# Split weights, an added mask and VectorE differences in a chain of an mLSTM layer and two feed-forward layers

## The chip, the core and the metric

The kernel runs on one core of a Trainium2 chip. The metric is the device time in microseconds (us). One execution was also profiled; its span runs from the first to the last instruction of the core.

## What is computed

The first stage is an mLSTM over 2 batches, 8 heads, 768 steps and 40 values a head. The kernel takes it in chunks of 128 steps: with the running maximum in hand, each chunk is a masked matrix of decays times scores, plus what the state carried into it. Two feed-forward layers follow, each 320 to 2048 to 320, all in float32.

```python
m_new = np.maximum(f_gate[:, :, t] + m, i_gate[:, :, t])
C = f_stab * C + i_stab * einsum('bhd,bhe->bhde', vt, kt)
y[:, :, t] = sigmoid(o_gate) * (C @ qt) / max(|n . qt|, 1)
x = y as (1536, 320)
h = x @ w_in;  g = h - tanh(h);  x = g @ w_out
h = x @ w_in2; g = h * tanh(softplus(h)); out = g @ w_out2
```

## The kernel before, in words

**Float32 products in parts.** Each float32 operand is held as a rounded high part and a low part, the difference of the two; a product is high x high, high x low and low x high. A weight tile holds 128 of the 2048 hidden columns: columns 0 to 255 are the first 256 input rows as two 128x128 blocks, columns 256 to 575 are the output weights, and columns 576 to 703 are the last 64 of the 320 input rows, put there twice, in partitions 0 to 63 and again in 64 to 127. `conv_w` makes the tile: two VectorE steps and a ScalarE step put the raw bits right (L202, L210, L214; L204 and L207 in the second layer), ScalarE rounds all 704 columns (L217), and VectorE writes the low parts in two pieces: 576 columns on 128 partitions (L220), then 128 columns on partitions 64 to 127 only (L221). That second piece overwrites the doubled rows' high parts, so that one 128x128 block holds high over low. The first tile's pieces run on GpSimd.

`transpose_x` makes xT for a chunk's activations: three transposes on TensorE, one rounding copy on ScalarE (L290, 128x3x128), one low part on VectorE (L293, 128x3x128). `mm1` then issues 8 matmuls a weight tile, and `mm2` 3 for each 128 tokens (L649 to L651).

**The order of work.** Layer 1 has 6 blocks of 2 chunks. The program walks a list of 48 tiles of layer 1: each block's first weights (8 for block 0, 10 for the others), then each block's rest. `attend` feeds the mLSTM of the next block in between, `lead1` the conversion of weights. A scheduler then sets each engine's order from priorities and buffers; the instructions of an engine run in that order. `with after(...)` adds order edges.

**A tile of layer 1** (`tile1`): two tanh and a square on ScalarE (L608 to L610), two products on VectorE (L613, L614), ReLU on ScalarE (L615), a predicated copy on VectorE (L617), and in `split_g` the rounding gh on ScalarE (L597) and the low part gl on GpSimd (L598). Layer 2 has the same difference on VectorE (L630).

**The mLSTM's mask.** `attention` builds the exponent of the decays in PSUM (nb) and takes its exponential on ScalarE into Dm (L361). For chunk 0 the causal mask is a further product into nb (L353: identity times cm, which is 2^100 above the diagonal), and the exponential of its negative is 0. For all later chunks GpSimd's affine_select (L363) zeroes Dm behind the exponential. VectorE then multiplies Dm by the scores (L389).

**Rows of gates.** `gates` scans all 768 steps. `rest_n` splits the rows of n and i of chunks 1 to 5 (640 columns of 16 partitions) into high parts on ScalarE (L163 from `copy_r`) and low parts on VectorE (L525), in the tile nr; from there small DMAs bring a chunk's rows to md and sd, which the product of L358 reads.

**Buffers.** The pool wp has 16 slots (tag "w"), first used by the gates' rows; the pool xp has 5 (tag "x") for the first 4 raw weight tiles and then xT.

Of the kernel before, what the change touches and what calls it, by code (L numbers as in the profile page):

```python
# [8 lines left out]
F32 = mybir.dt.float32  # L9
F32R = mybir.dt.float32r  # L10
U32 = mybir.dt.uint32
# [14 lines left out]
def kernel(  # L26
# [20 lines left out]
    HP = P // 2  # L47
    REM0, REM1 = 256 + DM, 256 + DM + 128
    HI0, HI1, OUT_HI, PCH = 0, 128, 256, REM0
    LO0, LO1, OUT_LO = WC, WC + 128, WC + 256  # L50
    WT = WC + 256 + DM

# [62 lines left out]
    EC = 1  # L115
    nr = once.tile([P, S - EC * L], F32R, name="nr")

# [56 lines left out]
    def load_w(n=1):  # L174
        for _ in range(n):
            if pending_loads:
                layer, f = pending_loads.pop(0)
                early = layer == 0 and f < ER
                t = (xp if early else rawp).tile(
                    [P, 2 * WC], U32, tag="x" if early else "raw", name="raw", bufs=NB - 1 if early else None  # L180
                )
                queued(
                    lambda: nc.sync.dma_start(out=t, in_=(w1, w2)[layer][f].bitcast(U32)), layer == 0 and f < CUT[0]
                )
                raw[layer, f] = t
# [3 lines left out]
    def conv_w(layer, f, first=(), behind=()):  # L189
# [29 lines left out]
        with after(scored[NP + 1] if (layer, f) == (0, CUT[0] - 1) else []):  # L219
            eng.tensor_tensor(w[:, WC:WT], in0=zf[:, 0:REM0], in1=wf[:, 0:REM0], op=ALU.subtract)  # L220
        lows[layer, f] = eng.tensor_tensor(w[64:P, REM0:REM1], in0=zf[64:P, REM0:REM1], in1=wf[64:P, REM0:REM1], op=ALU.subtract)  # L221
        wtile[layer, f] = w
# [54 lines left out]
    def new_xT(layer, bi):  # L277
        nt = len(blk[layer, bi]) * L
        p, m = (late.get("x", xp), M1) if layer == 0 else (x2pool(bi), M2)
        t = p.tile([P, 2, 3, m], F32R, tag="x", name="xT", bufs=len(supers[0]) if layer else 1 if p is not xp else NB - 1)  # L280
        xT[layer, bi] = tuple(t[:, n, :, 0:nt] for n in range(2))

    def transpose_x(layer, bi, pos):
        j = blk[layer, bi][pos]
        src = xo[:, j, :]
        t_ps = at_ps([P, 3, P], "xt")
        for n in range(3):
            x = nc.tensor.transpose(t_ps[:, n, :], src[:, n * P:(n + 1) * P], ident)  # L288
        hi, lo = (t[:, :, pos * L:(pos + 1) * L] for t in xT[layer, bi])
        chain[:] = [x, nc.scalar.activation(out=hi, in_=t_ps, func=AF.Copy)]  # L290

        def low():
            chain.append(nc.vector.tensor_tensor(lo, in0=t_ps, in1=hi.bitcast(F32), op=ALU.subtract))  # L293

        return low
# [23 lines left out]
    def attention(j):  # L319
# [18 lines left out]
        for hf in range(2):  # L338
# [18 lines left out]
            else:  # L357
                nc.tensor.matmul(flat, lhsT=sds[b], rhs=md_[:, hf].rearrange("p g s -> p (g s)"), start=True, stop=True)  # L358
# [109 lines left out]
    def gates():  # L468
# [45 lines left out]
        def rest():  # L514
            with after([first]):
                scans(L, S)
            return rest_n

        def rest_n():
            for n, t in enumerate((n_t, i_t)):  # L520
                t, hi, lo = t[:, EC * L:S], nr[64 * n:64 * n + BH], nr[64 * n + 32:64 * n + 32 + BH]
                with after(texp):
                    copy_r(0, hi, t)
                with after([lows[0, 1]]):
                    nc.vector.tensor_tensor(lo, in0=t, in1=hi.bitcast(F32), op=ALU.subtract)  # L525
            return rest_u
# [36 lines left out]

    segs = [(bi, 0, CUT[bi]) for bi in range(NB)] + [(bi, CUT[bi], NF) for bi in range(NB)]
    tiles = [(0, bi, f) for bi, f0, f1 in segs for f in range(f0, f1, NP)]
    half = len(tiles)
# [8 lines left out]
    def mm1(i):  # L575
        l, bi, fs, nt = span(i)
        t = ps_h.tile([P, MX], F32, tag="h", name="h")[:, 0:len(fs) * nt]
        xh, xl = xT[l, bi]
        pairs = [
            (HI0, xh, 0), (HI1, xh, 1), (HI0, xl, 0), (HI1, xl, 1), (LO0, xh, 0), (LO1, xh, 1), (PCH, xh, 2), (PCH, xl, 2),  # L580
        ]
        for k, f in enumerate(fs):
            w = wtile[l, f]
            for n, (o, x, kk) in enumerate(pairs):
                with after([] if n else hold):
# [47 lines left out]
    def mm2(i):  # L633
# [18 lines left out]
        if fs[-1] + 1 in ends_ or fs[-1] == NF - 1:  # L652
            more = l == 0 and fs[-1] + 1 > CUT[bi]
            for t, a in enumerate(accs.pop((l, bi))):
# [21 lines left out]
    late = {}  # L676

# [5 lines left out]
    def program():  # L683
# [297 lines left out]
```

## Time and profile before

| | us |
|---|---|
| median of 3 runs | 448.72 (448.59 to 448.79) |
| the profiled execution's own time | 447.9 |
| its span | 446.2 |
| TensorE busy in the span | 436.4 |
| VectorE busy | 305.4 |
| ScalarE busy | 283.5 |
| GpSimd busy | 99.2 |

In the profile PE is TensorE's matmuls, PEld its weight loads, DVE VectorE, ACT ScalarE, POOL GpSimd. L12 is line 12 of the kernel before. Matmuls overlap in the records, so a busy TensorE is not one at its peak; w_ps are matmuls on constants that nobody reads. The chain of waits follows the last instruction back to what released it, step by step. A window's row gives the busy time of each engine in that stretch.

### The profile page before, as it was taken

How to read it: one execution, taken by the hardware profiler on the slowest of the kernel's cores; microseconds unless marked ns; L12 is line 12 of the kernel's file. 1: busy time of each engine (PE TensorE's matmuls, PEld its weight loads, DVE VectorE, ACT ScalarE, POOL GpSimd, SP SyncE). 2: the span in 40 equal slices, each digit the busy share in tenths (PEclk: the TensorE clock that was granted, in tenths of full speed). 3: DMA queues.
4: the chain of work that ended last, by engine and by line, in shares of the span. 5: the costliest groups of instructions: out<-in, count | busy, mean ns of one | idle time of the engine just before them, and what ended most of it. 6: DMA issues, size and time to landing. Idle time of an engine off the chain costs nothing.

```text
span 446.2 us, 7979 instructions
## 1 busy us (share of the span) xinstructions
PE 436.4 (98%) x3114; PEld 399.5 (90%) x3114; DVE 305.4 (68%) x521; ACT 283.5 (64%) x519; POOL 99.2 (22%) x107
## 2 busy tenths in 40 slices
PE   9899989999999999999999999999999999999996
PEld 5657979899899999999999999999999888999996
DVE  7899999978899896578999987898522211211112
ACT  6687987485786858889889877666434322333331
POOL 2307235343452521333333331000000000000000
PEclk9999999999999999999999999999999999999999
DMA  8986526423244210002222110543010000100001
GB/s 247 368 301 206 187 62 226 125 70 95 62 151 136 66 67 0 1 2 66 65 67 66 65 66 0 195 132 128 0 60 0 1 1 1 42 18 0 1 0 59
DMA packets 22728, 38.03 MB, mean 85 GB/s; under 512 B 1348, under 2 KB 17028, under 8 KB 22692
## 3 DMA queue, kind: packets, MB, share of 16 engines
q1 hardware_dynamic: 22692, 37.54, 25.7%
q8 instruction: 24, 0.39, 0.4%
q14 instruction: 12, 0.10, 0.1%
HBM read 35.41 MB, written 1.97 MB: 84 GB/s over the span
## 4 chain that ended last, share of the span: by engine, by line
PE 86%; DVE 8%; ACT 4%; issue 1%; ACTq 0%; DVEq 0%
PE h L586 37%; PE acc L649 12%; PE acc L651 12%; PE acc L650 12%; PE pv L409 3%; PE sc L385 2%; PE w_ps L690 2%; PE it L396 2%; PE xt L288 2%; DVE g L613 1%; DVE t L614 1%; DVE g L617 1%; DVE Dm L389 1%; ACT raw L210 1%; PE nb L358 1%
## 5 line engine op out<-in xcount | busy, mean ns | idle before, releaser
L586 PE MATMUL h<-xT,w 128*128 128x256 f32 (+1 forms) x1152 | 205.8, 321 | 0.5 <-DVE w L220 0.2
L586 PEld LDWEIGHTS h<-xT,w 128*128 128x128 f32 x1152 | 168.7, 188 | 15.7 <-issue 0.9
L649 PE MATMUL acc<-w,gh 128*128 128x320 f32 x384 | 119.5, 312 | 0.6 <-ACT gh L597 0.4
L650 PE MATMUL acc<-w,gh 128*128 128x320 f32 x384 | 118.8, 310 | 0.0
L651 PE MATMUL acc<-w,gl 128*128 128x320 f32 x384 | 114.0, 310 | 0.0
L598 POOL TENSOR_TENSOR gl<-g,gh 128x512 fp32r<-128x512 f32 x48 | 62.5, 1303 | 139.1 <-ACT gh L597 134.1
L630 DVE TENSOR_TENSOR gl<-g,gh 128x512 fp32r<-128x512 f32 x48 | 33.2, 691 | 87.4 <-ACT g L629 87.2
L628 ACT ACTIVATE gh<-h 128x512 fp32r<-128x512 f32 x48 | 28.7, 598 | 78.1 <-PE h L586 78.0
L649 PEld LDWEIGHTS acc<-w,gh 128*128 128x128 f32 x384 | 72.2, 188 | 3.4 <-ACT gh L597 0.7
L650 PEld LDWEIGHTS acc<-w,gh 128*128 128x128 f32 x384 | 72.2, 188 | 2.4
L651 PEld LDWEIGHTS acc<-w,gl 128*128 128x128 f32 x384 | 70.4, 188 | 0.7 <-issue 0.4
L617 DVE COPY_PREDICATED g<-u,t 128x512 f32<-128x512 uint32 x48 | 39.3, 824 | 10.0 <-ACT u L615 9.6
L597 ACT ACTIVATE gh<-g 128x512 fp32r<-128x512 f32 x48 | 30.3, 632 | 22.8 <-DVE g L617 21.5
L613 DVE TENSOR_TENSOR g<-u,h 128x512 f32<-128x512 f32 x48 | 32.7, 680 | 13.8 <-ACT u L610 3.9
L615 ACT ACTIVATE u<-u,bias 128x512 f32<-128x512 f32 x48 | 34.8, 725 | 8.2 <-DVE g L613 8.2
L217 ACT ACTIVATE w<-raw 128x704 fp32r<-128x704 f32 x32 | 27.2, 861 | 10.8 <-DVE raw L214 10.5
L614 DVE TENSOR_TENSOR t<-h,t 128x512 f32<-128x512 f32 x48 | 32.8, 684 | 0.0
L214 DVE SCALAR_TENSOR_TENSOR raw<-raw 128x704 uint32<-128x704 uint32 x32 | 32.0, 1007 | 1.0 <-ACT raw L207 0.4
L220 DVE TENSOR_TENSOR w<-raw,w 128x576 fp32r<-128x576 f32 x31 | 29.1, 939 | 1.9 <-ACT w L217 1.8
L610 ACT ACTIVATE u<-u 128x512 f32<-128x512 f32 x48 | 30.4, 636 | 0.0
L608 ACT ACTIVATE u<-h 128x512 f32<-128x512 f32 x48 | 28.1, 585 | 1.3 <-PE h L586 1.3
L629 ACT ACTIVATE g<-h 128x512 f32<-128x512 f32 x48 | 28.5, 594 | 0.0
(108 smaller groups left out, 445.0 us busy)
## 6 DMA issues: line engine op xcount, KB each, us to landing
raw<-in_w_dram SPq DMA_DIRECT2D x32, 704.0 KB
qk_t<-in_qk_dram SPq DMA_DIRECT2D x12, 512.0 KB
kv_t<-in_kv_dram SPq DMA_DIRECT2D x12, 324.0 KB
out_dram<-xo SPq DMA_DIRECT2D x12, 160.0 KB
xo<-in_og_dram SPq DMA_DIRECT2D x2, 800.0 KB
xo<-in_og_dram SPq DMA_DIRECT2D x1, 320.0 KB
sd<-nr SPq DMA_DIRECT2D x20, 4.0 KB
md<-nr SPq DMA_DIRECT2D x10, 8.0 KB
```

The lines of the kernel that those rows point to most:

```text
L214: third[layer, f] = nc.vector.scalar_tensor_tensor(z, in0=z, scalar=3, in1=lo32, op0=ALU.logical_shift_left, op1=ALU.bitwise_or)
L586: y = nc.tensor.matmul(t[:, k * nt:(k + 1) * nt], lhsT=w[:, o:o + P], rhs=x[:, kk, :], start=(n == 0), stop=(n == len(pairs) - 1),)
L598: nc.gpsimd.tensor_tensor(gl, in0=g, in1=gh.bitcast(F32), op=ALU.subtract)
L610: squared[:] = [nc.scalar.activation(out=u, in_=u, func=AF.Square, scale=G_SA)]
L613: mark[:] = [nc.vector.tensor_tensor(g, in0=u, in1=h, op=ALU.mult)]
L614: nc.vector.tensor_tensor(t, in0=h, in1=t, op=ALU.subtract)
L615: relus[i] = nc.scalar.activation(out=u, in_=u, func=AF.Relu, bias=bias[:, 0:1])
L617: chosen[i] = nc.vector.copy_predicated(out=g, mask=u.bitcast(U32), data=t)
L630: mark.append(nc.vector.tensor_tensor(gl, in0=g, in1=gh.bitcast(F32), op=ALU.subtract))
L649: turn(lambda: nc.tensor.matmul(a, lhsT=gh[:, sl], rhs=wh, start=(f in ends_), stop=False))
L650: turn(lambda: nc.tensor.matmul(a, lhsT=gh[:, sl], rhs=wl, start=False, stop=False))
L651: turn(lambda: nc.tensor.matmul(a, lhsT=gl[:, sl], rhs=wh, start=False, stop=end))
```

## The change

Four edits. (1) The last 64 rows: the weight tile now rounds all 704 columns and writes one low part of all 704, on 128 partitions (high blocks HI0, HI1, PCH; low blocks LO0, LO1, PCL); xT holds five blocks rather than six, and the third holds the high part in partitions 0 to 63 and the low part in 64 to 127. So the low part of xT is two VectorE instructions: 64x128 in place, then 128x2x128. A weight tile still has 8 matmuls. (2) In chunk 1 (c equal to EC) the mask is the product with cm, once for each of its 4 nb tiles, and the affine_select goes. (3) gl of tiles 2 and 3 is on VectorE. (4) nr is split in two pieces: 256 columns (chunks 1 and 2) where all 640 were, 384 columns at the start of tile 4. The first 4 raw tiles move to the pool wp, and nr to the pool xp.

```diff
-    REM0, REM1 = 256 + DM, 256 + DM + 128
-    HI0, HI1, OUT_HI, PCH = 0, 128, 256, REM0
-    LO0, LO1, OUT_LO = WC, WC + 128, WC + 256
-    WT = WC + 256 + DM
+    HI0, HI1, OUT_HI, PCH = 0, 128, 256, 256 + DM
+    LO0, LO1, OUT_LO, PCL = WC, WC + 128, WC + 256, WC + 256 + DM
+    WT = 2 * WC
...
-    nr = once.tile([P, S - EC * L], F32R, name="nr")
+    nr = xp.tile([P, S - EC * L], F32R, tag="x", name="nr", bufs=NB - 1)
...
-                t = (xp if early else rawp).tile(
-                    [P, 2 * WC], U32, tag="x" if early else "raw", name="raw", bufs=NB - 1 if early else None
-                )
+                t = (wp if early else rawp).tile([P, 2 * WC], U32, tag="w" if early else "raw", name="raw")
...
-            eng.tensor_tensor(w[:, WC:WT], in0=zf[:, 0:REM0], in1=wf[:, 0:REM0], op=ALU.subtract)
-        lows[layer, f] = eng.tensor_tensor(w[64:P, REM0:REM1], in0=zf[64:P, REM0:REM1], in1=wf[64:P, REM0:REM1], op=ALU.subtract)
+            lows[layer, f] = eng.tensor_tensor(w[:, WC:WT], in0=zf, in1=wf[:, 0:WC], op=ALU.subtract)
...
-            chain.append(nc.vector.tensor_tensor(lo, in0=t_ps, in1=hi.bitcast(F32), op=ALU.subtract))
+            y = t[64:P, 2]
+            nc.vector.tensor_tensor(y, in0=t_ps[64:P, 2], in1=y.bitcast(F32), op=ALU.subtract)
+            chain.append(
+                nc.vector.tensor_tensor(t[:, 3:5], in0=t_ps[:, 0:2], in1=t[:, 0:2].bitcast(F32), op=ALU.subtract)
+            )
...
+                if c == EC:
+                    nc.tensor.matmul(
+                        nb, lhsT=identr, rhs=cm.rearrange("p (o s) -> p o s", o=1).to_broadcast([P, HG, L]), start=False,
+                        stop=True,
+                    )
...
-            if c >= EC:
+            if c > EC:
                 nc.gpsimd.affine_select(
...
+        def split(c0, c1, x, y):
+            to = slice((c0 - EC) * L, (c1 - EC) * L)
+            for n, t in enumerate((n_t, i_t)):
+                hi, lo = nr[64 * n:64 * n + BH, to], nr[64 * n + 32:64 * n + 32 + BH, to]
+                t = t[:, c0 * L:c1 * L]
+                with after(x):
+                    copy_r(0, hi, t)
+                with after(y):
+                    nc.vector.tensor_tensor(lo, in0=t, in1=hi.bitcast(F32), op=ALU.subtract)
+
         def rest_n():
+            split(EC, EC + 2, texp, [lows[0, 1]])
+            late["n"] = lambda: split(EC + 2, NCH, [rounded[CUT[0] // NP - 1]], [chosen[CUT[0] // NP - 1]])
...
-        pairs = [
-            (HI0, xh, 0), (HI1, xh, 1), (HI0, xl, 0), (HI1, xl, 1), (LO0, xh, 0), (LO1, xh, 1), (PCH, xh, 2), (PCH, xl, 2),
-        ]
+        pairs = [(HI0, 0), (HI1, 1), (PCH, 2), (HI0, 3), (HI1, 4), (LO0, 0), (LO1, 1), (PCL, 2)]
...
-        nc.gpsimd.tensor_tensor(gl, in0=g, in1=gh.bitcast(F32), op=ALU.subtract)
+        eng = nc.vector if i in (2, 3) else nc.gpsimd
+        eng.tensor_tensor(gl, in0=g, in1=gh.bitcast(F32), op=ALU.subtract)
...
             if i == n_s:
                 fill.clear()
+                late["n"]()
```

The scheduler also moves instructions. Three places follow; line numbers of the changed kernel are 10 to 15 higher than those of the kernel before for the same operation.

GpSimd's queue from the first tile's low part to the first state update, before (w is the weight tile, dl and wv the mLSTM's state operands):

```order
L220 TENSOR_TENSOR w<-raw,w 128x576
L221 TENSOR_TENSOR w<-raw,w 64x128
L598 TENSOR_TENSOR gl<-g,gh 128x512
L363 AFFINE_SELECT Dm<-Dm 128x512 x3
L167 TENSOR_SCALAR dl<-Dm 128x8
L363 AFFINE_SELECT Dm<-Dm 128x512
L373 TENSOR_TENSOR wv<-kv_t,dl 128x328
L167 TENSOR_SCALAR dl<-Dm 128x8
L373 TENSOR_TENSOR wv<-kv_t,dl 128x328
L598 TENSOR_TENSOR gl<-g,gh 128x512
L438 TENSOR_TENSOR C<-C,dec 40x4x41 x2
L598 TENSOR_TENSOR gl<-g,gh 128x512
```

and in the changed kernel:

```order
L217 TENSOR_TENSOR w<-raw,w 128x704
L613 TENSOR_TENSOR gl<-g,gh 128x512 x2
L166 TENSOR_SCALAR dl<-Dm 128x8
L382 TENSOR_TENSOR wv<-kv_t,dl 128x328
L166 TENSOR_SCALAR dl<-Dm 128x8
L382 TENSOR_TENSOR wv<-kv_t,dl 128x328
L447 TENSOR_TENSOR C<-C,dec 40x4x41 x4
```

The four selects of chunk 1 are gone, two low parts of g stand ahead of the state operands, and the third and fourth gl are not in the queue.

VectorE's queue from tile 2's first product to the second product of chunk 1's first batch, before:

```order
L613 TENSOR_TENSOR g<-u,h 128x512
L614 TENSOR_TENSOR t<-h,t 128x512
L389 TENSOR_TENSOR Dm<-sc,Dm 128x512
L221 TENSOR_TENSOR w<-raw,w 64x128
L389 TENSOR_TENSOR Dm<-sc,Dm 128x512
L220 TENSOR_TENSOR w<-raw,w 128x576
L401 TENSOR_TENSOR hv<-it,uT 128x328
L617 COPY_PREDICATED g<-u,t 128x512
L413 TENSOR_TENSOR hv<-hv,pv 128x328
```

and in the changed kernel:

```order
L628 TENSOR_TENSOR g<-u,h 128x512
L629 TENSOR_TENSOR t<-h,t 128x512
L199 TENSOR_SCALAR raw<-raw 128x704
L632 COPY_PREDICATED g<-u,t 128x512
L211 SCALAR_TENSOR_TENSOR raw<-raw 128x704
L398 TENSOR_TENSOR Dm<-sc,Dm 128x512 x2
L613 TENSOR_TENSOR gl<-g,gh 128x512
L410 TENSOR_TENSOR hv<-it,uT 128x328
L217 TENSOR_TENSOR w<-raw,w 128x704
L422 TENSOR_TENSOR hv<-hv,pv 128x328
```

The predicated copy stands earlier, and gl of tile 2 is between the scores and the state's part.

ScalarE's queue around the gh of tile 3, before:

```order
L290 ACTIVATE xT<-xt 128x3x128
L597 ACTIVATE gh<-g 128x512
L210 ACTIVATE raw<-raw 128x704 x3
L361 ACTIVATE Dm<-nb 128x512 x2
L608 ACTIVATE u<-h 128x512
```

and in the changed kernel:

```order
L288 ACTIVATE xT<-xt 128x3x128
L611 ACTIVATE gh<-g 128x512
L162 ACTIVATE nr<-n_all 16x384
L162 ACTIVATE nr<-gi 16x384
L207 ACTIVATE raw<-raw 128x704 x3
L370 ACTIVATE Dm<-nb 128x512 x2
```

The second piece of nr stands between gh and three weight conversions.

## Rows read from the trace of the kernel before

**Rows 1.** The page, parts 1 and 2: totals; VectorE in 40 slices of 11.2 us.

```profile
PE 436.4 (98%) x3114; PEld 399.5 (90%) x3114; DVE 305.4 (68%) x521; ACT 283.5 (64%) x519; POOL 99.2 (22%) x107
...
DVE  7899999978899896578999987898522211211112
```

**Rows 2.** Engines by window: stretch, length, busy us (count) of each, clock, DMA.

```profile
20.00:30.00 10.00, 9.51 (x83) 5.98 (x83) 9.54 (x17) 9.77 (x19) 0.00 (x0) 1.00 0.88 281
...
40.00:50.00 10.00, 9.93 (x91) 9.11 (x89) 9.84 (x16) 7.16 (x12) 5.25 (x8) 1.00 0.56 187
...
60.00:70.00 10.00, 9.98 (x87) 9.48 (x86) 9.41 (x15) 10.00 (x21) 5.89 (x7) 1.00 0.30 97
...
100.00:110.00 10.00, 10.00 (x91) 9.88 (x91) 7.98 (x16) 6.43 (x12) 3.84 (x3) 1.00 0.26 70
```

**Rows 3.** Chain of waits in order of time: start, us, engine, tile, line, count.

```profile
7.34 0.29 PE nb L353
...
17.81 1.49 DVE xo L423
...
60.00 1.59 ACT raw L210 x2
...
86.96 0.50 DVE xo L423
...
87.60 0.41 PE xt L288 x2
```

**Rows 4.** Timeline of VectorE with GpSimd idle: start, us, engine, line, operation, form.

```profile
21.01 0.96 DVE L202 TENSOR_SCALAR raw<-raw 128x704 uint32<-128x704 uint32 x2
...
28.50 0.75 DVE L220 TENSOR_TENSOR w<-raw,w 128x576 fp32r<-128x576 f32 x1
...
29.29 0.29 DVE L221 TENSOR_TENSOR w<-raw,w 64x128 fp32r<-64x128 f32 x1
...
31.95 0.75 DVE L617 COPY_PREDICATED g<-u,t 128x512 f32<-128x512 uint32 x1
...
32.60 0.88 DVE L214 SCALAR_TENSOR_TENSOR raw<-raw 128x704 uint32<-128x704 uint32 x1
...
54.06 0.16 DVE L419 TENSOR_TENSOR den<-hv,den 128x8 f32<-128x8 f32 x1
...
56.70 0.55 DVE L293 TENSOR_TENSOR xT<-xt,xT 128x384 fp32r<-128x384 f32 x1
```

**Rows 5.** Timeline of GpSimd, same columns.

```profile
17.52 1.43 POOL L220 TENSOR_TENSOR w<-raw,w 128x576 fp32r<-128x576 f32 x1 [3.46 <-ACT w L217]
...
36.68 2.75 POOL L363 TENSOR_SCALAR_AFFINE_SELECT Dm<-Dm 128x512 f32<-128x512 f32 x3 [1.05 <-ACT Dm L361]
...
50.53 1.30 POOL L598 TENSOR_TENSOR gl<-g,gh 128x512 fp32r<-128x512 f32 x1 [4.00 <-ACT gh L597]
```

**Rows 6.** Timeline of VectorE beside a running GpSimd operation, same columns.

```profile
37.10 0.61 DVE L221 TENSOR_TENSOR w<-raw,w 64x128 fp32r<-64x128 f32 x1
...
37.73 1.21 DVE L214 SCALAR_TENSOR_TENSOR raw<-raw 128x704 uint32<-128x704 uint32 x1
...
38.87 1.20 DVE L617 COPY_PREDICATED g<-u,t 128x512 f32<-128x512 uint32 x1
...
40.10 1.18 DVE L220 TENSOR_TENSOR w<-raw,w 128x576 fp32r<-128x576 f32 x1
...
50.61 1.23 DVE L419 TENSOR_TENSOR den<-hv,den 128x8 f32<-128x8 f32 x1
...
59.13 2.07 DVE L202 TENSOR_SCALAR raw<-raw 128x704 uint32<-128x704 uint32 x2
```

**Rows 7.** Groups by line and form: xcount, busy us, mean ns, idle before.

```profile
L630 DVE TENSOR_TENSOR gl<-g,gh 128x512 fp32r<-128x512 f32 x48 | 33.2, 691 | 87.4 <-ACT g L629 87.2
...
L525 DVE TENSOR_TENSOR nr<-gi,nr 16x640 fp32r<-16x640 f32 x1 | 0.8, 819 | 0.0
...
L163 ACT ACTIVATE nr<-gi 16x640 fp32r<-16x640 f32 x1 | 0.7, 734 | 0.0
```

More of the change, by code (lines that the diff above doesn't have):

```diff
@@ L279, in new_xT @@
         p, m = (late.get("x", xp), M1) if layer == 0 else (x2pool(bi), M2)
-        t = p.tile([P, 2, 3, m], F32R, tag="x", name="xT", bufs=len(supers[0]) if layer else 1 if p is not xp else NB - 1)
-        xT[layer, bi] = tuple(t[:, n, :, 0:nt] for n in range(2))
+        t = p.tile(
+            [P, 5 * m], F32R, tag="x", name="xT", bufs=len(supers[0]) if layer else 1 if p is not xp else NB - 1
+        )
+        xT[layer, bi] = t.rearrange("p (k t) -> p k t", k=5)[:, :, 0:nt]
     def transpose_x(layer, bi, pos):
@@ L288, in transpose_x @@
             x = nc.tensor.transpose(t_ps[:, n, :], src[:, n * P:(n + 1) * P], ident)
-        hi, lo = (t[:, :, pos * L:(pos + 1) * L] for t in xT[layer, bi])
-        chain[:] = [x, nc.scalar.activation(out=hi, in_=t_ps, func=AF.Copy)]
+        t = xT[layer, bi][:, :, pos * L:(pos + 1) * L]
+        chain[:] = [x, nc.scalar.activation(out=t[:, 0:3], in_=t_ps, func=AF.Copy)]
         def low():
-            chain.append(nc.vector.tensor_tensor(lo, in0=t_ps, in1=hi.bitcast(F32), op=ALU.subtract))
+            y = t[64:P, 2]
[3 more added lines that the diff above has]
+            )
         return low
@@ L357, in attention @@
             else:
-                nc.tensor.matmul(flat, lhsT=sds[b], rhs=md_[:, hf].rearrange("p g s -> p (g s)"), start=True, stop=True)
+                nc.tensor.matmul(
+                    flat, lhsT=sds[b], rhs=md_[:, hf].rearrange("p g s -> p (g s)"), start=True, stop=c > EC
+                )
+                if c == EC:
+                    nc.tensor.matmul(
+                        nb, lhsT=identr, rhs=cm.rearrange("p (o s) -> p o s", o=1).to_broadcast([P, HG, L]), start=False,
+                        stop=True,
+                    )
             dh = Dm[:, 4 * hf:4 * hf + 4, :]
@@ L517, in rest @@
             return rest_n
-        def rest_n():
[L520 to L525, printed above, removed]
+        def split(c0, c1, x, y):
[7 more added lines that the diff above has]
+                    nc.vector.tensor_tensor(lo, in0=t, in1=hi.bitcast(F32), op=ALU.subtract)
+        def rest_n():
+            split(EC, EC + 2, texp, [lows[0, 1]])
+            late["n"] = lambda: split(EC + 2, NCH, [rounded[CUT[0] // NP - 1]], [chosen[CUT[0] // NP - 1]])
             return rest_u
@@ L564 @@
     segs = [(bi, 0, CUT[bi]) for bi in range(NB)] + [(bi, CUT[bi], NF) for bi in range(NB)]
+    late = {}
     tiles = [(0, bi, f) for bi, f0, f1 in segs for f in range(f0, f1, NP)]
@@ L577, in mm1 @@
         t = ps_h.tile([P, MX], F32, tag="h", name="h")[:, 0:len(fs) * nt]
-        xh, xl = xT[l, bi]
-        pairs = [
-            (HI0, xh, 0), (HI1, xh, 1), (HI0, xl, 0), (HI1, xl, 1), (LO0, xh, 0), (LO1, xh, 1), (PCH, xh, 2), (PCH, xl, 2),
-        ]
+        x = xT[l, bi]
+        pairs = [(HI0, 0), (HI1, 1), (PCH, 2), (HI0, 3), (HI1, 4), (LO0, 0), (LO1, 1), (PCL, 2)]
         for k, f in enumerate(fs):
             w = wtile[l, f]
-            for n, (o, x, kk) in enumerate(pairs):
+            for n, (o, kk) in enumerate(pairs):
                 with after([] if n else hold):
@@ L674, in mm2 @@
                     nc.sync.dma_start(out=out[b * S + c * L:b * S + (c + 1) * L, :], in_=o)
-    late = {}
     def x2pool(bi):
```

## The prediction

> **What bounds the kernel now.** I began with the page: TensorE is busy for 436.4 of 446.2 us, VectorE for 305.4, but VectorE's slices show where that lies, 9s and 8s up to about slice 8 and again later [rows 1]. TensorE's record is no guide in the first part, since its matmuls overlap and constants fill its gaps, so I read the windows next. Between 20 and 30 us both VectorE (9.54 of 10) and ScalarE (9.77) are full; between 40 and 50 VectorE has 9.84 and ScalarE 7.16; between 60 and 70 ScalarE has 10.00 and VectorE 9.41; from 100 VectorE has 7.98 and TensorE goes on without a gap [rows 2]. The chain of waits says the same: up to 87.5 us it goes through VectorE and ScalarE, and where VectorE's last gating of the third block ends (86.96 + 0.50), the transposes take over on TensorE at 87.60 [rows 3]. Behind that TensorE has work to the end, and this work does not change. So the change is worth what it moves that hand-over, and every other term is covered. The full clock is granted throughout (1.00 in each window [rows 2]), so no term is priced at a lower one.
>
> The sum is made against the profiled execution, 447.9 us with a span of 446.2. The median shown is 448.72, 0.8 above it, and I carry the difference over.
>
> **Prices.** One low part of 704 columns: 576 take 0.75 and 128 columns on half the partitions 0.29 [rows 4], so a column costs (0.75 - 0.29)/448 = 1.03 ns and 704 columns 0.75 + 0.13 = 0.88. That saves 0.16 a tile; by proportion to 576 columns it would be 0.92 and save 0.12. xT's low part takes 0.55 for 384 columns [rows 4]. In two pieces it is 0.29 plus 256 columns, 0.37 by proportion, 0.42 on the line from 128 to 384; I take 0.42, so a transposed chunk costs 0.16 more. gl on VectorE: 0.69 [rows 7]. The rows of gates cost 0.82 each on VectorE and 0.73 on ScalarE for 640 columns [rows 7]; by proportion 384 columns cost 0.49 and 0.44, 256 columns 0.33 and 0.29. A share of fixed cost could bring 384 columns up to 0.82 and 0.73, which bounds them.
>
> The fourth price is the contention. VectorE's operations take longer beside GpSimd's. Against the same operations alone [rows 4], the four during chunk 1's selects (2.75 us for three, then one more [rows 5]) show 0.61 for 0.29, 1.21 for 0.88, 1.20 for 0.75 and 1.18 for 0.75 [rows 6]: 0.32 + 0.33 + 0.45 + 0.43 = 1.5 us. During tile 2's gl on GpSimd (1.30 us [rows 5]) a den of 8 columns takes 1.23 where one alone takes 0.16 [rows 4, 6]: 1.1 us. During tile 3's gl, two raw steps take 2.07 where two alone take 0.96 [rows 4, 6]: again 1.1. So a gl on GpSimd has cost VectorE 1.1, and on VectorE it costs 0.69.
>
> The Trainium skill (SBUF, "Who interferes with whom") says that a VectorE instruction with two SBUF inputs and a GpSimd instruction that reads SBUF exclude each other for the whole instruction. The den agrees with it (1.23 beside 1.30); the operations beside the selects lose less than a select's length each.
>
> **Part by part, up to the hand-over.** The order of VectorE up to that gating holds the same instructions before and after but for the ones priced here, ten of the low parts of weights among them.
>
> First stretch, to 35 us. Four low parts (-0.6), nr's first piece (-1.0 on VectorE, -0.9 on ScalarE) and two xT (+0.3). But ScalarE is as full as VectorE there, and the same weight conversions, tanh and squares stand on it; I count these savings at nothing. What counts is at the start: GpSimd's low part of the first tile is one piece of 704 columns, 0.3 longer than 576 by proportion to its 1.43 [rows 5], and VectorE's gating at 17.81 lasts until just behind the first of GpSimd's pieces now (1.49, to 19.30; 17.52 + 1.43 = 18.95) [rows 3, 5]. That is +0.3 on the chain, and with one xT low part in front of the next conversion about **+0.4**.
>
> Second stretch, 35 to 58 us, where VectorE is full and ScalarE is not: the selects' contention -1.5; three low parts of weights -0.5; tile 2's gl 0.69 - 1.1 = -0.4. Together **-2.4**. The four mask products cost TensorE 0.29 each [rows 3], 1.2 in all; TensorE has constants to multiply in this stretch and waits for Dm anyway, so they are covered; were they not, 1.2 comes back. The wait for GpSimd between the exponential and the scores goes too, and what is late next is the exponential.
>
> Third stretch, 58 to 67 us: the chain runs on ScalarE, of which the raw conversions at 60.00 are a piece [rows 3], and the second piece of nr stands in front of them, two copies of 0.44: **+0.9**. VectorE in the same stretch: tile 3's gl 0.69 - 1.1, nr's two low parts +1.0, two xT low parts +0.3, two weights' -0.3, together +0.6, beside ScalarE's 0.9.
>
> Fourth stretch, 67 to 88 us: one low part of weights, **-0.2**.
>
> At no cost: the loads (SP issues the same number of DMAs, the first four raw tiles in the same order), since the pool wp has 16 slots, of which the gates' scans have given up several before the first weights are written; xT's fifth block waits for nr's last small DMAs, which follow chunk 4's nb products long before its transposes. In layer 2 the shorter low parts and the longer xT parts lie beside a TensorE that never waits.
>
> Sum: 0.4 - 2.4 + 0.9 - 0.2 = -1.3. The profiled execution would take 446.6, the median 448.7 - 1.3 = **447.4 us**.
>
> **Bounds.** If the savings of the first stretch count (-0.6 - 1.0 + 0.3 in place of the +0.4), and ScalarE's 0.9 is hidden, the sum is -1.3 - 2.4 - 0.2 = -3.9: 444.8. If GpSimd's remaining operations meet VectorE as often as the removed ones did, the contention terms vanish: +0.4, then -0.5 + 0.7 in the second stretch, +0.9, -0.2 make +1.3: 450.0.
>
> **The rivals.** *No change.* VectorE is the full engine, and the change puts more operations on it. If tile 2's gl is paid in full (0.69 rather than -0.4, so +1.1) while the selects' contention goes, the sum is -1.3 + 1.1 = -0.2: 448.5. For it: the operations that a gl held up were short and had others behind them that could have met the next GpSimd operation. Against: the den's row [rows 6]. The Trainium skill (Perfetto Trace Analysis, "Optimizing Scalar/DVE Operations") speaks for this side: it says that work may go off a saturated VectorE, to GpSimd even, though the shared port may leave nothing gained, and the change goes the other way. The rows here side with its second half, 1.1 against 0.69. Chance 0.27.
>
> *Slower.* The GpSimd operations that remain (two gl, two wv, two C updates) now come at other moments, and each finds a VectorE operation with two SBUF inputs. From the point at which they hold VectorE as long as the selects and the two gl did, 2.6 us in the second stretch, what remains is the longer start and the 0.9 on ScalarE: 450.0. For it: wv and C have shown 0.4 of such delay already (1.18 at 40.10 lasts beyond the select). Against: there are six fewer GpSimd operations. Chance 0.17.
>
> *A larger gain.* ScalarE is not the bound in the first stretch: it also sat waiting for TensorE and VectorE within it, and its order is changed. Then 444.8, chance 0.15. That the change does not do what it says is excluded by the queues shown: the selects and the two gl have left GpSimd's.
>
> **How the numbers follow.** The forecast has 0.41. A measurement can tell about 0.2% from no change, 0.9 us. The forecast (447.4, own range 446.5 to 447.8) and the larger gain are faster: 0.56. No change 0.27, slower 0.17. The range runs from 445.0, near the larger gain, to 449.5, between no change and slower, and leaves out about 2 in 10.
>
> **What would show it.** Right: the gating that ended at 87.46 ends about 1.3 earlier; no VectorE operation beside a select before 55 us; gl on VectorE at 0.69; the weight's low part at 0.88; two copies of some 0.44 on ScalarE in front of the raw conversions, in the chain. Wrong: idle time of VectorE between 35 and 58 us waiting for ScalarE, or operations stretched beside wv and C; a hand-over at the old time. The forecast fails altogether if TensorE has gaps behind 90 us that it did not have.

## The result, and the profile after

The changed kernel takes 455.07 us (median of 6 runs, 453.12 to 455.98), the kernel before 448.69 beside it (6 runs). The ratio is 1.0138, 95% interval 1.0117 to 1.0159: slower by 6.4 us. The profiled execution took 455.68 us, its span is 454.0. Five of the six runs show a mean granted clock of 0.992, the sixth, the fastest, 0.999.

First the page, totals, VectorE's slices, now of 11.35 us, and PEclk, the clock that TensorE was granted in each slice, in tenths of its full speed (9 is 90% or more). From here on L12 is line 12 of the kernel whose trace is shown. (The line numbers of the changed kernel do not all lie 10 to 15 above those of the kernel before, as said ahead: they run from 3 lower to 15 higher, so that L217, ScalarE's rounding before, is now the low part.)

```profile
PE 440.5 (97%) x3118; PEld 402.4 (89%) x3118; DVE 298.6 (66%) x518; ACT 283.8 (63%) x521; POOL 93.5 (21%) x100
...
DVE  7976899868898788558899987898422222211112
...
PEclk9989999989999999999999999999999999999999
```

VectorE has 298.6 us of work in place of 305.4 and GpSimd 93.5 in place of 99.2 [rows 1]: the change took away what it should. But VectorE's slices have 8s, a 7 and a 6 where 9s stood, and in two slices the granted clock is not full. Two of the windows of [rows 2], and four short ones (stretch, length, busy time and count of PE, PEld, DVE, ACT and POOL, granted clock, DMA share, GB/s):

```profile
20.00:30.00 10.00, 9.83 (x77) 5.89 (x76) 7.48 (x15) 7.84 (x15) 0.00 (x0) 0.83 0.90 293
40.00:50.00 10.00, 10.00 (x73) 7.93 (x72) 6.49 (x11) 7.67 (x13) 3.35 (x5) 1.00 0.42 140
...
88.00:90.00 2.00, 1.16 (x7) 0.64 (x5) 2.00 (x5) 1.26 (x2) 1.10 (x1) 1.00 0.00 0
90.00:92.00 2.00, 0.00 (x0) 0.00 (x0) 2.00 (x3) 0.00 (x0) 1.82 (x2) 1.00 0.01 4
92.00:94.00 2.00, 1.68 (x11) 1.71 (x12) 0.95 (x4) 0.52 (x2) 0.00 (x0) 0.89 0.00 0
94.00:96.00 2.00, 2.00 (x27) 1.61 (x27) 0.08 (x1) 0.49 (x1) 0.00 (x0) 0.50 0.00 0
```

Between 40 and 50 us VectorE has 6.49 of 10 (before 9.84): the engine that I took for the bound waits. From 88 to 92 TensorE does nothing for 2.84 us of 4, and behind that its granted clock is 0.89 in one window and 0.50, the lower of its two levels (1.2 of 2.4 GHz), in the next. Between 20 and 30 it is 0.83. Summed over windows of 2 us up to 14 us before the end, TensorE is idle for 6.3 us before and 10.1 after; (1 - clock) times its busy time is 0.0 before and 3.4 after; the span less both is 439.9 and 440.5. So the 7.8 us of the span are 3.8 of standing still, 3.4 of half clock and 0.6 of anything else. This sorts the time; it does not yet say which of it ends the kernel later.

The prices, in the changed kernel's timeline of VectorE (start, us, engine, line, operation, form), answer to [rows 3, 4, 6, 7]:

```profile
17.69 1.77 DVE L432 SCALAR_TENSOR_TENSOR xo<-xo,den 128x320 f32<-128x320 f32 x1
19.49 0.29 DVE L292 TENSOR_TENSOR xT<-xt,xT 64x128 fp32r<-64x128 f32 x1
19.80 0.42 DVE L294 TENSOR_TENSOR xT<-xt,xT 128x256 fp32r<-128x256 f32 x1
...
39.67 0.87 DVE L211 SCALAR_TENSOR_TENSOR raw<-raw 128x704 uint32<-128x704 uint32 x1
...
50.32 0.78 DVE L613 TENSOR_TENSOR gl<-g,gh 128x512 fp32r<-128x512 f32 x1
...
64.00 0.69 DVE L613 TENSOR_TENSOR gl<-g,gh 128x512 fp32r<-128x512 f32 x1
64.73 0.55 DVE L536 TENSOR_TENSOR nr<-n_all,nr 16x384 fp32r<-16x384 f32 x1
```

xT's two pieces take 0.29 and 0.42 as priced, gl 0.78 and 0.69 (priced at 0.69), a low part of three chunks of the rows 0.55 (0.49), and a low part of 704 columns 0.89 in the row at 44.05 below (0.88). GpSimd's first low part takes 1.70 from 17.41 us (before 1.43 from 17.52 [rows 5]), and the gating beside it 1.77, 0.28 more than before: +0.3 was the price. No raw step between 37 and 44 us is stretched any more (0.87 at 39.67). Each instruction costs about what I said. The loss is in the order.

Where it lies, four landmarks say: the ends of the second gating of the first, second and third block, and the end of the span. Two of the rows are new, one of VectorE before and one after:

```profile
54.49 0.49 DVE L423 SCALAR_TENSOR_TENSOR xo<-xo,den 128x320 f32<-128x320 f32 x1
```

```profile
57.69 0.49 DVE L432 SCALAR_TENSOR_TENSOR xo<-xo,den 128x320 f32<-128x320 f32 x1
```

| stretch, us | before | after |
|---|---|---|
| to the first block's second gating | 19.30 | 19.46 |
| from there to the second block's | 35.68 | 38.72 |
| from there to the third block's, the hand-over | 32.47 | 34.83 |
| from there to the end of the span | 358.75 | 360.99 |

So 0.2, 3.0, 2.4 and 2.2 us, the last with 1.7 of half clock in it.

**Two places where the order shows.** The first is in the middle. VectorE's timeline there, and in brackets the idle time ahead and what ended it:

```profile
44.05 0.89 DVE L217 TENSOR_TENSOR w<-raw,w 128x704 fp32r<-128x704 f32 x1 [3.51 <-ACT w L214]
```

ScalarE's:

```profile
40.22 1.09 ACT L370 ACTIVATE Dm<-nb 128x512 f32<-128x512 f32 x2 [1.60 <-PE nb L364]
...
43.15 0.87 ACT L214 ACTIVATE w<-raw 128x704 fp32r<-128x704 f32 x1
```

TensorE's:

```profile
38.96 0.75 PE L600 MATMUL h<-xT,w 128*128 128x256 f32 x5
39.55 0.39 PE L360 MATMUL nb<-md,sd 128*128 128x512 f32 x1
```

The nb products and the exponentials before:

```profile
34.18 0.86 PE L358 MATMUL nb<-md,sd 128*128 128x512 f32 x3
```

```profile
36.01 1.57 ACT L361 ACTIVATE Dm<-nb 128x512 f32<-128x512 f32 x3
```

Before, TensorE's first three nb products of chunk 1 stood behind four products of tile 2's first weight and ran at 34.18 us; now they stand behind five of its second weight and run at 39.55. So the exponentials start at 40.22 in place of 36.01, the weight's copy behind them at 43.15, and VectorE stands idle for 3.51 us for it. That VectorE's idle time is itself on the path is not shown: the profile's chain of waits runs on TensorE from 34.8 to 56.6 us in the changed kernel.

The second is at the hand-over. VectorE:

```profile
88.38 0.20 DVE L429 RECIPROCAL den<-den 128x8 f32<-128x8 f32 x1
88.49 0.70 DVE L632 COPY_PREDICATED g<-u,t 128x512 f32<-128x512 uint32 x1
89.06 1.25 DVE L427 TENSOR_SCALAR den<-hv 128x8 f32<-128x8 f32 x1
90.22 0.48 DVE L431 TENSOR_TENSOR xo<-hv,xo 128x320 f32<-128x320 f32 x1
90.63 1.55 DVE L432 SCALAR_TENSOR_TENSOR xo<-xo,den 128x320 f32<-128x320 f32 x1
...
92.52 0.49 DVE L432 SCALAR_TENSOR_TENSOR xo<-xo,den 128x320 f32<-128x320 f32 x1
```

TensorE:

```profile
92.32 0.41 PE L286 MATMUL xt<-ident,xo 128*128 128x128 f32 x2 [2.59 <-DVE den L428]
...
94.15 0.47 PE L665 MATMUL acc<-w,gh 128*128 128x320 f32 x1
```

The third block's first gating (L432 at 90.63) has its reciprocal at 88.38, and could follow at once. But VectorE's queue holds tile 8's masked copy (88.49) and two steps of the other chunk in front of it. The copy holds the queue for 0.6 us; the greater part is that two gl on GpSimd (2.93 us from 88.89) lie beside what follows: a den of 8 columns takes 1.25 in place of 0.16, the gating 1.55 in place of 0.49. The transposes, which read xo, come at 92.32 (the row names the step behind the gating), after 2.59 us without a matmul, and then a product takes 0.47 where it took 0.31. The second gating, which my sum hung on, ends at 93.01, not at 86.2.

The Trainium skill (PSUM — Partial Sum Buffer, "Engine vs sequencer instructions") says that the queues of ScalarE, VectorE and GpSimd are strictly first in, first out. The rows agree: the gating, whose reciprocal ends at 88.58, waits out the copy and the two steps.

### The profile page after: what moved, and what is told of

Read it like the earlier page. It is cut to its first block, busy times and chain, and to the rows that moved or that the text cites. A ratio compares the mean times of both kernels' runs of the same rounds, so it can differ in the third digit from the quotient of the medians.

```text
span 454.0 us, 7982 instructions
## 1 busy us (share of the span) xinstructions
PE 440.5 (97%) x3118; PEld 402.4 (89%) x3118; DVE 298.6 (66%) x518; ACT 283.8 (63%) x521; POOL 93.5 (21%) x100
## 4 chain that ended last, share of the span: by engine, by line
PE 87%; DVE 8%; ACT 3%; issue 2%; DVEq 0%; ACTq 0%
PE h L600 38%; PE acc L664 12%; PE acc L666 12%; PE acc L665 12%; PE pv L418 3%; PE sc L394 3%; PE w_ps L703 2%; PE it L405 2%; PE xt L286 2%; DVE t L629 1%; DVE g L632 1%; DVE g L628 1%; PE nb L360 1%; DVE xo L432 1%; ACT raw L207 1%
## 5 line engine op out<-in xcount | busy, mean ns | idle before, releaser
L613 POOL TENSOR_TENSOR gl<-g,gh 128x512 fp32r<-128x512 f32 x46 | 61.1, 1328 | 128.6 <-ACT gh L611 124.8
L630 ACT ACTIVATE u<-u,bias 128x512 f32<-128x512 f32 x48 | 35.1, 730 | 6.7 <-DVE g L628 6.7
L217 DVE TENSOR_TENSOR w<-raw,w 128x704 fp32r<-128x704 f32 x31 | 33.0, 1068 | 5.9 <-ACT w L214 5.9
L211 DVE SCALAR_TENSOR_TENSOR raw<-raw 128x704 uint32<-128x704 uint32 x32 | 29.7, 930 | 3.0 <-ACT raw L207 2.4
L624 ACT ACTIVATE t<-h 128x512 f32<-128x512 f32 x48 | 28.7, 599 | 0.0
```

The costliest lines, as they stand in the source:

```text
L217: lows[layer, f] = eng.tensor_tensor(w[:, WC:WT], in0=zf, in1=wf[:, 0:WC], op=ALU.subtract)
L613: eng.tensor_tensor(gl, in0=g, in1=gh.bitcast(F32), op=ALU.subtract)
L630: relus[i] = nc.scalar.activation(out=u, in_=u, func=AF.Relu, bias=bias[:, 0:1])
```

## The experiments

18 kernels ran, each beside the kernel before on the same chip; where two of them are compared, the ratios to the kernel before count for more than the times. Two theories were set against each other at first. *Start*: the longer low part at the start and the clock behind it make the loss. *Sum of orders*: every edit lets the scheduler write another order of all engines, and the waits in that order make it.

### Each edit alone, and each edit taken back

The four edits are the parts of the diff shown ahead; their tell-tale lines:

```diff
...
halves
+    HI0, HI1, OUT_HI, PCH = 0, 128, 256, 256 + DM
+    LO0, LO1, OUT_LO, PCL = WC, WC + 128, WC + 256, WC + 256 + DM
mask
+            if c > EC:
gl
+        eng = nc.vector if i in (2, 3) else nc.gpsimd
rows
+            split(EC, EC + 2, texp, [lows[0, 1]])
+                late["n"]()
```

a1 to a4 put one of them into the kernel before, u1 to u4 take one out of the changed kernel. The two moves between the pools go with the halves and were not tried alone.

> Kernel before with the halves alone (weights' and xT's low parts). Theory 'start': the first tile's low part on GpSimd as one piece and xT's low part in two hold the first blocks up, TensorE idles before 20 us and before about 90 us, its granted clock falls there, and most of the 6.4 us comes from this edit: 451 to 454. Theory 'sum of orders': no edit alone carries the loss; what counts is that ScalarE and VectorE wait for one another between 30 and 62 us when several edits move together: this one alone 447.5 to 449.5, with at most the first fall of the clock. My prediction's prices: 448.7 + 0.4 - 0.5 - 0.2 = 448.4.

> Kernel before with the mask as a product for chunk 1 alone. Prediction's price: contention of the selects gone, -1.5: 447.2. If the product is on the path: +1.2, 449.9. Theory 'start': no loss, 447 to 449. Theory 'sum of orders': chunk 1 comes earlier and displaces work of the first tiles on ScalarE, 448 to 451.

> Kernel before with gl of tiles 2 and 3 on VectorE alone. Prediction's price: -0.4 in the second stretch, -0.4 beside ScalarE in the third: 448.3. If a gl is paid in full: +0.7 to +1.4, 449.4 to 450.1. Theory 'start': within 1 of 448.7. Theory 'sum of orders': within 1 of 448.7 too.

> Kernel before with the rows of gates in two pieces alone. Prediction's price: +0.9 in the third stretch, with up to -1 saved in the first: 448.7 to 449.6. Theory 'start': 448.7 to 449.6. Theory 'sum of orders': the second piece stands in front of tile 4's raw conversions on ScalarE and in front of the gating on VectorE, 449.6 to 451.

> Changed kernel with the halves taken back (weights and xT as before; mask, gl and rows as changed). Theory 'start': the start is that of before, both falls of the clock go, 447 to 449. Theory 'sum of orders': the waits between 30 and 62 us remain, 450 to 453.

> Changed kernel with the selects back for chunk 1. Prediction's price: 455.1 + 1.5 = 456.6. Theory 'start': 455 to 457. Theory 'sum of orders': the order of the first tiles comes back with them, 451 to 454.

> Changed kernel with all gl on GpSimd. Prediction's price: 455.1 + 0.4 = 455.5. Theory 'start': 455 to 456. Theory 'sum of orders': 453 to 455.

> Changed kernel with the rows of gates in one piece. Prediction's price: 455.1 - 0.9 = 454.2. Theory 'start': 454 to 455. Theory 'sum of orders': the third stretch gets its old order, 452 to 454.

| edit | alone: us, ratio to before | the change without it: us, ratio to before |
|---|---|---|
| halves | 451.60, 1.0058 (1.0038 to 1.0079) | 457.77, 1.0187 (1.0140 to 1.0233) |
| mask | 449.51, 1.0012 (0.9996 to 1.0027) | 455.09, 1.0142 (1.0106 to 1.0178) |
| gl | 447.98, 0.9975 (0.9960 to 0.9990) | 453.37, 1.0108 (1.0092 to 1.0123) |
| rows | 451.79, 1.0062 (1.0044 to 1.0080) | 450.28, 1.0041 (1.0028 to 1.0054) |

Alone, the halves and the rows lose about 3 us each, gl gains 0.8. In company the halves gain 2.7 by the medians (the two intervals overlap), and gl loses 1.7. *Start* falls: without the halves the changed kernel has its old start and is the slowest of these. The rows lose in both columns, 3.0 and 4.8, where I had priced +0.9. An edit's work is the same in both columns, and what it is worth is not (for the halves the 5.5 us between the columns are clear of the noise): it hangs on what the other edits do to the order.

The mask, my largest gain (-1.5), gives nothing that can be measured in either column. The trace of the mask alone shows where the saving went. Two of VectorE's rows there:

```profile
42.90 1.29 DVE L396 TENSOR_TENSOR Dm<-sc,Dm 128x512 f32<-128x512 f32 x2 [1.17 <-PE sc L392]
...
85.72 0.49 DVE L430 SCALAR_TENSOR_TENSOR xo<-xo,den 128x320 f32<-128x320 f32 x1
```

The copy beside which a select stood takes 0.78 in place of 1.20, and VectorE then waits for TensorE's scores: between 34 and 58 us the waits ahead of its rows add up to 3.5 us, before to 0.7. And the third block's second gating ends at 86.21, 1.2 us earlier than before (87.45), which is what my whole sum forecast, but TensorE has 1074 acc products (those with the output weights) behind it in place of 1061, and the time does not fall.

### Constants in TensorE's first gap

TensorE stands idle for 1.54 us ahead of the second transposes, and in the changed kernel its clock falls to 0.50 between 22 and 24 us. Four more constant products fill the gap, and leave every engine's order as it is; a fifth lets the scheduler write another.

```diff
-        keep(4, chain[0])
+        keep(8, chain[0])
```

> Changed kernel with eight constant products in place of four behind the first transposes; the order of every engine is otherwise the changed kernel's. Theory 'clock': TensorE's gap ahead of the second transposes shrinks from 1.54 to about 0.7 us, the granted clock stays 1.00 between 20 and 26 us (0.97, 0.50 and 0.68 now), and the 1.7 us that TensorE loses there come back: 453 to 453.7; if the second fall, behind 92 us, goes too, 452 to 453. Rival 'waits': the clock comes back, but the products wait for conversions anyway: 454.5 to 455.5.

> Changed kernel with nine constant products there: one more than in the run before, but with it the scheduler writes another order on all engines (hundreds of rows on TensorE stand elsewhere). Theory 'order': the work is the same, the order alone moves the time: over 1.5 us off the run with eight, either way. Rival 'work': within 0.7 us of it.

With eight: 455.24 us (1.0146). The clock between 20 and 26 us is 1.00, and the time does not move: a fall of the same 1.7 us stands between 60 and 66 instead, the gap at 88 to 92 is still there (2.88 us idle), and the second fall too. So the change does not lose by where its first fall stands. (That the constants moved it is not shown: in the last run of this study, which has four of them, it stands at 60 us as well.) Whether the fall at 22 us costs time stays open: from the first block's second gating to the second block's it is 38.72 us with the fall and 37.23 in both profiles without it, but with eight constants the times show none of these 1.5 us. With nine: 453.38 us (1.0103). One constant product more, 0.26 us by the four that took 1.04, and 1.9 us less: in that order TensorE is idle for 0.9 us between 80 and 100, not 3.0, and in the profiled run the clock holds throughout. By the sum used above standing still is the same as with eight (8.3 and 8.2 us in all) and the half clock is gone (0.0 and 3.4). *Sum of orders* stands, with the clock behind the gaps as a part of it.

### Chunk 1's nb products where they were

```diff
...
+                with after(nbs[-1:] if (i, k, n) == (2, 0, 5) else [] if n else hold):
...
+                    with after(nbs[-1:] if (i, k, t) == (0, 0, 0) else []):
```

(nbs holds the last product of the first three nb; the second line is that of tile 0's first acc product.)

> Changed kernel with chunk 1's first three nb products held ahead of the sixth product of tile 2's first weight, where the kernel before has them (34.18 us against 39.55). Theory 'order': the exponentials of chunk 1 start about 3 us earlier, VectorE's idle 3.51 us at 44 us goes, the second block's gatings end 2 to 3 us earlier (58.2 now): 452 to 453.5. Rival 'rows': what counts is the second piece of the rows of gates behind 62 us and TensorE's gap at 90 us, and they remain: 454.3 to 456.

> Kernel before with the halves alone (451.6), chunk 1's first three nb products held where the kernel before has them. Theory 'nb': the halves cost through this place (exponentials of chunk 1 at 39.7 against 36.5 us): 448.5 to 449.5. Rival 'next wait': the second block's second gating and the idle TensorE ahead of it remain, as they did when the changed kernel got its nb back: 450.5 to 452.

In the changed kernel: 454.40 us (1.0130). The exponentials come 3.0 us earlier, as meant, the second block's first gating ends at 53.50 in place of 55.30, but its second at 59.48 in place of 58.18. The median is 0.7 us lower, and the two intervals overlap: a gain is not shown. In the kernel with the halves alone: 454.86 (1.0148), slower still, but nothing follows from it: in its profile TensorE waited 1.33 us for a load of q and k at 10 us, and ran at half clock from 14 to 24 us; all four runs show a mean clock of 0.976 to 0.984. Why the halves alone cost 2.8 us stays open; part of it goes with half clock, since of that kernel's ten runs the three at a mean clock of 0.996 took 450.0 to 450.8 us, the five at 0.987 or 0.989 452.0 to 452.8.

### The place of the rows' second piece

```diff
...
+            if i == n_s + 2:
                 late["n"]()
...
-            late["n"] = lambda: split(EC + 2, NCH, [rounded[CUT[0] // NP - 1]], [chosen[CUT[0] // NP - 1]])
+            late["n"] = lambda: split(EC + 2, NCH, [rounded[CUT[0] // NP + 1]], [chosen[CUT[0] // NP + 1]])
```

> Kernel before with the rows of gates in two pieces alone (451.8), the second piece two tiles later, where ScalarE has idle time (about 75 us in place of 60). Theory 'place': the 1.1 us on ScalarE ahead of tile 4's raw conversions and the 1.1 us on VectorE between the raw steps made the loss; here they lie beside idle time: 448.3 to 449.5. Rival 'VectorE': any 1.1 us on VectorE ahead of the third block's gatings costs as much wherever it stands: 450.8 to 452.3.

> Changed kernel with the second piece of the rows two tiles later. Theory 'place': with it the changed kernel is that without two pieces (450.3) less what two pieces give when placed late (0.9 on the kernel before): 449 to 450.5. Rival 'order': the place of the piece is one of many things that the order hangs on, and the changed kernel stays behind: 452 to 456.

> Kernel before with gl of tiles 2 and 3 on VectorE and the rows in two pieces, the second late; weights, xT and masks as before. If the two gains (0.8 and 0.9) add: 447.0 to 447.4. If they free the same wait, or the order shifts: 447.7 to 449.

> The same with the mask as a product too: the changed kernel but for the halves and the place of the second piece. Theory 'place': without the early piece the falls of the clock at 50 to 62 us (457.8 with the early piece) go, and the sum of the single edits holds: 447 to 448.5. Rival 'order': 450 and over.

ScalarE's timeline with the rows alone:

```profile
59.77 0.51 ACT L163 ACTIVATE nr<-n_all 16x384 fp32r<-16x384 f32 x1
60.30 0.52 ACT L163 ACTIVATE nr<-gi 16x384 fp32r<-16x384 f32 x1
60.85 2.38 ACT L210 ACTIVATE raw<-raw 128x704 f32<-128x704 f32 x3
```

The same with the second piece late:

```profile
59.22 2.37 ACT L210 ACTIVATE raw<-raw 128x704 f32<-128x704 f32 x3
...
75.95 0.51 ACT L163 ACTIVATE nr<-n_all 16x384 fp32r<-16x384 f32 x1
```

The two copies (the later kernel has the second of them behind the row shown) put the raw conversions from 59.25 (before) to 60.85, and the third block's two gatings, staggered before (84.02 and 87.45), now end at 87.66 and 89.33; with the piece late the conversions start at 59.22 and the time is 447.97 us, ratio 0.9979 (0.9970 to 0.9989). The same work, two tiles later, is 3.8 us: the place, with the order that follows from it, made that edit's loss. But the changed kernel gains at most 0.8 by it (454.26, 1.0126, and the two intervals overlap); gl and the late rows together, worth 0.8 and 0.9 alone, take 450.07 (1.0037); and with the mask 456.82 (1.0173). My sums failed here as they had in the prediction.

### One waiting copy on VectorE

The two slowest kernels, the changed one without the halves (457.8) and the one with gl, the mask and the late rows (456.8), run at half clock from 50 to 62 us. VectorE's timeline in the one at 456.8 us:

```profile
48.65 0.73 DVE L632 COPY_PREDICATED g<-u,t 128x512 f32<-128x512 uint32 x1 [2.07 <-ACT u L630]
49.27 1.28 DVE L396 TENSOR_TENSOR Dm<-sc,Dm 128x512 f32<-128x512 f32 x2
```

ScalarE's:

```profile
45.97 1.28 ACT L264 ACT_TABLE_LOAD   x1
47.27 0.74 ACT L264 ACTIVATE xo<-xo 128x640 f32<-128x640 f32 x1
47.91 0.71 ACT L630 ACTIVATE u<-u,bias 128x512 f32<-128x512 f32 x1
```

TensorE's:

```profile
50.00 3.64 PE L416 MATMUL pv<-kv_t,Dm 128*128 128x41 f32 x16 [2.41 <-DVE Dm L396]
```

Tile 2's masked copy waits for a relu (L630) that stands behind an activation table load and a sigmoid; chunk 1's score products wait behind the copy, TensorE behind those, and after 2.41 us its products take 3.64, where the kernel before has 1.98. One edge puts the copy behind the score products. A like edge, in the changed kernel, puts tile 8's masked copy behind the third block's first gating:

```diff
...
f1: kernel with gl, mask and late rows
+        with after([gated[NP + 1]] if joint else scored[NP + 1] if i == 2 else []):
...
f2: changed kernel
+        with after([gated[NP + 1]] if joint else [gated[2 * NP]] if i == 8 else []):
             chosen[i] = nc.vector.copy_predicated(out=g, mask=u.bitcast(U32), data=t)
```

> The run with gl, mask and late rows but without the halves (456.8), tile 2's masked copy on VectorE held behind chunk 1's last two score products. Theory 'gap and clock': the copy waits for a relu that stands behind an activation table load and a sigmoid on ScalarE, the score products wait behind it, TensorE stands still for 2.41 us from 47.6 us and runs at half the clock until 62: with the copy behind, gap and half clock go, and 4 to 7 us come back: 450 to 453. Rival 'order': the clock is not what ends the time, 455 to 457.

> Changed kernel with tile 8's masked copy on VectorE held behind the third block's first gating. Theory 'gap and clock': the gating ended at 92.18 us, behind the copy and behind operations that two gl on GpSimd stretch (1.25 and 1.55 in place of 0.16 and 0.49); it comes about 2 us earlier, TensorE's gap from 89.7 to 92.3 us shrinks below 1 us, the granted clock stays 1.00 from 92 to 98, and 2 to 3.5 us come back: 451.5 to 453. Rival 'later': TensorE has gaps behind 100 us that take them up: 454.3 to 455.5.

f1: 449.30 us in place of 456.82, ratio 1.0025 (1.0007 to 1.0042). f2: 451.38 in place of 455.07, ratio 1.0062 (1.0046 to 1.0077). Windows of the slow kernel:

```profile
48.00:50.00 2.00, 0.00 (x0) 0.00 (x0) 1.35 (x3) 1.83 (x5) 0.18 (x1) 0.97 0.58 158
50.00:54.00 4.00, 4.00 (x18) 4.00 (x19) 2.54 (x5) 3.41 (x6) 0.00 (x0) 0.50 0.60 186
54.00:58.00 4.00, 4.00 (x21) 4.00 (x19) 1.92 (x7) 0.26 (x1) 1.11 (x2) 0.50 0.13 52
```

The same stretch of f1:

```profile
48.00:50.00 2.00, 2.00 (x20) 2.00 (x20) 1.90 (x4) 1.73 (x4) 0.01 (x1) 1.00 0.64 184
50.00:54.00 4.00, 4.00 (x34) 4.00 (x34) 3.90 (x11) 3.98 (x7) 1.26 (x2) 1.00 0.92 262
```

Windows of f2 at and behind the hand-over:

```profile
90.00:92.00 2.00, 1.92 (x40) 1.76 (x41) 1.58 (x5) 1.38 (x4) 0.57 (x1) 1.00 0.00 0
...
94.00:96.00 2.00, 2.00 (x17) 1.95 (x16) 1.85 (x6) 2.00 (x7) 0.55 (x1) 1.00 0.17 65
```

VectorE's timeline in f2:

```profile
87.77 0.19 DVE L429 RECIPROCAL den<-den 128x8 f32<-128x8 f32 x1
...
88.36 1.57 DVE L432 SCALAR_TENSOR_TENSOR xo<-xo,den 128x320 f32<-128x320 f32 x1
89.86 0.75 DVE L632 COPY_PREDICATED g<-u,t 128x512 f32<-128x512 uint32 x1
```

TensorE's:

```profile
90.08 0.53 PE L286 MATMUL xt<-ident,xo 128*128 128x128 f32 x3 [0.98 <-DVE xo L432]
```

In f1 TensorE has no gap between 48 and 54 us and the clock is 1.00. Of the 8.7 us between the two profiled spans (455.8 and 447.1), 6.8 are half clock that is gone and 1.2 standing still, by the sum used above, though later rows of the order differ too. Beside their own kernels before, the medians of the two differ by 7.3 us, the ratios by 6.6.

In f2 the gating comes at 88.36, the transposes at 90.08 after 0.98 us in place of 2.59, the clock behind them stays 1.00, and 3.4 us of the 6.4 are back, each beside its kernel before: about the 1.6 us of gap and the 1.7 of half clock behind it. The gating itself is still stretched (1.57), beside the one gl that is left there (1.31 us from 88.28): the second gl comes later because tile 8's copy does. By the landmarks f2 takes 20.35, 37.23, 33.83 and 358.59 us: the stretch up to the hand-over is 1.0 shorter than the changed kernel's, and the one behind it 2.4, where it is again as quick as before.

What is left, 2.8 us by the ratio, lies ahead of the hand-over: its stretches are 1.0, 1.5 and 1.4 us longer than before, of which the first varies by as much from profile to profile (18.90 to 20.44 us in all profiles of this study but one). The rows' second piece and the nb products may have a part in the others (0.8 and 0.7 by the medians, each tried alone, neither clear of the noise); a kernel with all of these mended was not run.

## Why the prediction was wrong

- **Prices**: right, as shown: 0.89, 0.71, 0.69 to 0.78, 0.28 for the longer start; the rows' copies and low parts took 0.07 and 0.06 more each (0.51 and 0.55).
- **First stretch, savings counted at nothing**: right. With the rows alone, tile 0's masked copy ends at 32.30 in place of 32.70, for 0.8 us less work of VectorE on the rows (0.41 and 0.42 in place of twice 0.82), but at the second block's second gating nothing is left of it (55.51, before 54.98).
- **Second stretch, -2.4**: wrong, and this is the first step that failed: "up to 87.5 us it goes through VectorE and ScalarE". The chain of waits of the kernel before does not. Between 35 and 58 us 16.4 us of it are TensorE's, 5.4 VectorE's and 1.4 ScalarE's. Two of its rows there (start, us, engine, tile, line, count):

```profile
43.24 1.16 PE sc L385 x14
...
49.91 1.75 PE pv L409 x16
```

  Between 40 and 50 VectorE was busy for 9.84 of 10 us, and for most of this time it was not what the end of the stretch waited for. The den that tile 2's gl stretched from 50.61 to 51.84 [rows 6] lies beside the second of these rows, so off the chain; the selects' 1.5, taken away alone, became waits for TensorE's scores. In the changed kernel the waits came on top: VectorE stood idle for 3.5 of 10 us between 40 and 50.
- **Third stretch, +0.9**: the mechanism was right (two copies ahead of the raw conversions: they started 1.6 us later), the size wrong: 3.0 alone, since the two chunks' gatings lost their stagger behind it.
- **The second step that failed**, and the one that made it a loss as far as the runs show, is the sentence under the whole sum: "The order of VectorE up to that gating holds the same instructions before and after but for the ones priced here". It holds the same instructions in another sequence, and so do TensorE and ScalarE. I priced each instruction where it had stood. The rows of the order, shown ahead of the prediction, had to be read for what now stands in front of each gating and each nb, and they were read for what was gone. Of the exponential the prediction says itself that it is late next; it gives that no price, and the exponential comes 4.2 us later (40.22, before 36.01). At the hand-over one edge that moves one copy gives 3.4 us back.
- **"Behind that TensorE has work to the end, and this work does not change"**: wrong too. Behind the hand-over the changed kernel takes 2.2 us more, 1.7 of it at half clock; and with the mask alone the hand-over came 1.2 us earlier with more work behind it, at no gain.
- **"So no term is priced at a lower" clock**: wrong as a consequence. Two gaps of TensorE, of 1.54 us (1.25 before) and of 2.59, were followed by matmuls at half clock, 3.4 us in all. The part at 94 us lies in the stretch behind the hand-over, which is 2.4 us shorter in f2, where the clock stays full; of the part at 22 us it stays open whether it cost time in the end.
- **The rivals**: "slower" had GpSimd's remaining operations holding VectorE, from 35 to 58 us. There it did not show: no raw step is stretched, and VectorE waits instead. But it does occur at the hand-over, at 89.06 and 90.63 (1.25 and 1.55 beside two gl), 2.2 us more than the same operations alone, on the way to the gating; in f2, with the copy behind, one of them, 1.57, is still there. The sign by which the forecast "fails altogether", gaps of TensorE behind 90 us, is what happened.

## What to carry to other kernels

Where a scheduler writes the order, the work that an edit takes away says little: look for what now stands in front of the operation that the bound engine waits for, and hold that place with an edge before judging the edit. One edge on one copy was worth 3.4 and about 7 us here, more than any of the four edits alone. And read the chain of waits through the whole stretch that a term is priced in: an engine that is busy for 9.84 of 10 us need not be the one that is waited for. Test an edit's worth with its place varied (the rows: 451.8 or 448.0), and a theory of orders with an edit that adds next to no work (one more constant: 1.9 us). Two of the 18 beat both kernels, and both are small: gl of tiles 2 and 3 on VectorE alone (447.98) and the rows in two pieces with the second late (447.97).

## What the runs showed of the hardware

- Half clock can last. In the kernel at 456.8 us TensorE is shown busy all the time from 50 to 62 us (two of the windows stand above), and the granted clock stays 0.50. VectorE is busy for 2.54 and 1.92 us of the first two windows of 4, ScalarE for 3.41 and 0.26.
- A gap of the same length is not always followed by a fall. Ahead of the second transposes TensorE stands still for 1.54 us in the changed kernel, and for 1.54 and 1.55 in the kernel with the halves alone and in the changed one without the rows; the granted clock falls to 0.50 in the first, and stays 1.00 from 20 to 26 us in the other two.
- The same program does not always fall. One of the changed kernel's six runs, at a mean clock of 0.999, took 453.12 us, 2.2 less than the median of the other five (455.31, all at 0.992); in the profiled one of these the two falls come to 3.4. In the kernel before, 38 runs at a mean clock of 0.996 have a median of 448.90, 25 at 0.999 one of 448.58, and five at 0.992 one of 448.63: at most 0.3 us for a difference of 0.003 of 446, or 1.3. So a fall can cost less than its length. That it costs only where TensorE is waited for would fit this; no run here shows it by itself.
